# Output stages on VectorE alone, larger transfers and another spacing of attention bursts in a fused sparse-attention and max-feed-forward kernel

## The chip, the cores and the metric

One core of one Trainium2 chip. The metric is device time in microseconds for one execution; the kernel before was run three times, and one further execution was profiled. Besides PE (TensorE, with its weight loads PEld) the core has VectorE (DVE), ScalarE (ACT), GpSimd (POOL) and SyncE (SP), and 16 DMA engines.

## The reference

Attention with 8 batches, 8 heads, 576 positions and 64 channels, then a feed-forward layer with a maximum over three weights:

```python
mask_local = (rel >= 0) & (rel < stride)                      # heads 0..3, stride = 32
mask_strided = (rel >= 0) & (pos[None, :] % stride == pos[:, None] % stride)   # heads 4..7
attn = softmax(where(mask, scale * q @ k.T, -1e9))
x = (attn @ v).transpose(0, 2, 1, 3).reshape(4608, 512)
h = np.maximum(np.maximum(x @ w1, x @ w2), x @ w3)            # [4608, 768]
return h @ w_out                                              # [4608, 512]
```

All is float32.

## The kernel before

Float32 products are made of three products of parts: each operand is split into a high part (a cast, on ScalarE) and a low part (the operand less its high part, on VectorE or GpSimd), and PE adds high·high, high·low and low·high in a PSUM bank. There are two such banks, used in turn (`bank()`).

**Attention** goes by units: a unit is two heads of a batch, 32 units, in each batch two strided ones and then two local ones. A unit passes `scores` (PE), `less_maximum` (DVE), `exponentials` (ACT), `probabilities` and `transposed` (DVE), `values` (PE), and `leading` and `rest`, copies to the token blocks. `burst(n)` does the values of unit n, the scores of unit n+1, the v load of n+2, the copies of n, the q and k load of n+3, and the maximum of n+1. The rest of unit n+1 follows in the next steps. A strided unit's v comes in four transfers of 32 rows (L280).

**Tokens.** Chunk one (512 tokens) is in an opening whose order stands in a string of steps (`OPENING`). Chunk two (512 tokens; loop at L714) has 18 steps of a first product (`ff_in`, `ff_max`: j = i // 3, weight i % 3) and 4 of the output (`ff_out`, `ff_store`); `first_bursts` says which step begins with which burst. Beside it `build_sums`, `build_mix`, `build_high` and `build_low` make sums of weights, mostly on GpSimd, for nine quads in the DRAM tensor `scratch`; `sums_at` says when.

The other 3584 tokens go in four **supers**, each of two blocks of 448 tokens. A super has nine quads of seven products (a Strassen-like scheme; operands A11, S1, S2, S4, S3, A12, A22), so 63 products k = 0 to 62, each of six matmuls of 448 (`product`, L762). The weight operand of each product is a stream of 256 KB loads from `scratch`, issued by SP with nine buffers (`load_next`, L661). In supers 0 to 3, 6, 6, 4 and 0 bursts go between the products (`COUNTS`), at k = 0, 10, 20 and so on (`before`), and the rest of a unit's attention two to five products later (`after`). Between products ScalarE copies banks (`snap`, L800), GpSimd adds and VectorE takes the maxima into `h_all` (L814).

**The output stage** of a super has seven tiles of 128 tokens, 18 matmuls of 512 each (`out_part`, L847). For each, `split` makes the parts of h: the high one on ScalarE (L837), the low one mostly on GpSimd (L838); `store` copies the bank on ScalarE (L853) and sends it off on ScalarE's own DMA queue (L855). Between tiles stands a piece of `conversion(s + 1)`, which makes the seven operands of the next super's x: casts on ScalarE (L673), low parts on VectorE, two of them on GpSimd (L676), and four differences of blocks on VectorE (L679). Conversion 0 runs beside the output steps of chunk two, whose stores are at L557 and L558.

What sets the order: every engine works through its instructions in the order in which they are written (`pin`). SP issues all loads and the stores to `scratch`, in order; ScalarE issues the stores of the output. The compiled program has eight DMA semaphores, taken in turn over both queues: each transfer waits until the one eight before it has landed, and the engine that issues it waits with it.

Of the kernel before, what the change touches and what calls it, by code (L numbers as in the profile page):

```python
# [33 lines left out]
PAIRED = 1  # L34
# [37 lines left out]
def fused_kernel(ctx, tc, qT, kT, qk_loc, qk_str, v_loc, v_str, m_loc, m_str, w1, w2, w3, w_out, out):  # L72
# [183 lines left out]
    def load_v(n):  # L256
        if n >= len(units):
            return
        b, p = units[n]
        if n in (2, 3):  # L260
            vt = io_early.tile([P, 2 * (MB + 1) * D], F32, name="v_t", bufs=2)
        else:
            vt = io.tile([P, 2 * MS * D], F32, name="v_t", bufs=2)
        if p < 2:

            v_of[n] = v = vt[:, : 2 * (MB + 1) * D].rearrange("p (h m d) -> p h m d", h=2, m=MB + 1)
            last = 3 * MB
            for j in range(3):
                pin(nc.sync.dma_start(out=v[32 * j : 32 * (j + 1)], in_=v_loc[b, p, :32, :, j * MB : (j + 1) * MB + 1, :]))
                yield  # L270
            pin(nc.sync.dma_start(out=v[96:, :, : NT - last, :], in_=v_loc[b, p, :32, :, last:, :]))
            yield
            pin(nc.sync.dma_start(out=v[96:, :, NT - last, :], in_=v_loc[b, p, 32:, :, NT - 1, :]))
            yield
        else:
            v_of[n] = v = vt.rearrange("p (h m d) -> p h m d", h=2, m=MS)
            for j in range(4):

                rows = NI if b < PAIRED else 32
                pin(nc.sync.dma_start(  # L280
                    out=v[32 * j : 32 * j + rows], in_=v_str[b, p - 2, :rows, :, j * MS : (j + 1) * MS, :]
                ))
                yield
# [282 lines left out]
    def build_sums(q):  # L566

        _, j, i = builds[q]
        to = scratch[q].rearrange("p n (l f) -> p n l f", l=2)
        for n in range(2):  # L570
            pin(nc.sync.dma_start(out=to[:, A12 : A11 + 1, n], in_=halves(kept[i, j].bitcast(F32)[:, n])))
        pin(nc.sync.dma_start(out=to[:, A22], in_=kept[i, j + 1].bitcast(F32)[:, :, :256]))
        if q % 3 == 0:
            both = swp.tile([P, 2, 512], F32, name="sums_low")
            a = [both[:, n] for n in range(2)]
        else:
            a = [wk.tile([P, 512], F32, name="work") for _ in range(2)]
        a_of[q] = a
        for x, jj, engine in zip(a, (j, j + 1), (nc.gpsimd, nc.gpsimd)):
            parts = kept[i, jj].bitcast(F32)  # L580
            pin(engine.tensor_tensor(out=x, in0=parts[:, 0], in1=parts[:, 1], op=ALU.add))
# [31 lines left out]
    for step in LOADS.split():  # L613
        if step[0] == "w":
            load_weights(1)
        else:
            if step not in begun_loads:
                begun_loads[step] = {"q": load_qk, "v": load_v}[step[0]](int(step[1:]))
            next(begun_loads[step])
# [18 lines left out]

    def burst(n, exponents_later=True):
# [15 lines left out]
    def load_next():  # L657
        if to_load:
            _, q, m = to_load.pop(0)
            w = second["wst"].tile([P, 2, 256], F32R, name="w_stream")  # L660
            pin(nc.sync.dma_start(out=w.bitcast(F32), in_=scratch[q][:, m].rearrange("p (l f) -> p l f", l=2)))  # L661
            stream.append(w)

    half = lambda blk, k: blk[:, 2:4, :] if k == 1 else blk[:, 0:2, :]
# [1 line left out]
    def conversion(s):  # L666
# [5 lines left out]
        def high(m, src):  # L672
            pin(nc.scalar.copy(out=x[m][:, 0], in_=src))  # L673

        def low(m, src, engine=nc.vector):
            pin(engine.tensor_tensor(out=x[m][:, 1], in0=src, in1=x[m][:, 0].bitcast(F32), op=ALU.subtract))  # L676

        def less(to, a, b):
            pin(nc.vector.tensor_tensor(out=to, in0=a, in1=b, op=ALU.subtract))  # L679
# [26 lines left out]
    x1.close()  # L706
    late = ExitStack()
    shp.append(late.enter_context(tc.tile_pool(name="sums", bufs=2)))
    first_bursts = {1: 8, 4: 9, 6: 10, 9: 11, 12: 12, 14: 13, 17: 14, 19: 15}
    sums_at = {-2: 1, 0: 2, 3: 3, 5: 4, 7: 5, 9: 6, 11: 7, 14: 8}  # L710
    coming, since = None, 0
    convert = iter(())
    paired_queries(9)
    for i in range(3 * NJ + CH // P):  # L714
        if i in first_bursts:
            coming, since = burst(first_bursts[i]), i
        if i < 3 * NJ:
            ff_in(1, i // 3, i % 3)
        else:
# [2 lines left out]
            exponentials(coming)  # L722
        if coming and i == since + 1:
            probabilities(coming)
        if i < 3 * NJ:
            ff_max(1, i // 3, i % 3)
        else:
            ff_store(1, i - 3 * NJ)
        if coming and i == since + 1:
            transposed(coming)  # L730
            if (coming + 1) % 4 in (0, 1):
                paired_queries(coming + 1)
            coming = None
        if i >= 3 * NJ:
            next(convert, None)
            load_next()
            load_next()
        if i - 3 in sums_at:
# [17 lines left out]
    def supers():  # L756
# [9 lines left out]

        def before(s, k):

            if k % 10 == 0 and k // 10 < COUNTS[s]:
                running[:] = [burst(16 + sum(COUNTS[:s]) + k // 10), k]  # L770

        def after(s, k):

            if running and running[0]:
# [6 lines left out]
                if k == since + 5 and n + 1 < len(units) and (n + 1) % 4 in (0, 1):  # L781
                    paired_queries(n + 1)

        def quad(s, q):
# [45 lines left out]

        halves_of, outs = {}, {}

        def split(t, j0, j1, engine):
# [3 lines left out]
            pin(nc.scalar.copy(out=to[:, 0, j0:j1], in_=src))  # L837
            pin(engine.tensor_tensor(out=to[:, 1, j0:j1], in0=src, in1=to[:, 0, j0:j1].bitcast(F32), op=ALU.subtract))  # L838

        def out_part(t, j0, j1):  # L840
            if t not in outs:
# [16 lines left out]
        for s in range(NSUPER):  # L858
            for q in range(9):
                quad(s, q)  # L860
                if q == 7:
                    split(0, 0, 4, nc.gpsimd)
                    split(1, 0, 4, nc.gpsimd)
            split(2, 0, 4, nc.gpsimd)
            split(0, 4, 6, nc.vector)
            split(1, 4, 6, nc.vector)
            split(2, 4, 6, nc.gpsimd)
            convert = conversion(s + 1) if s + 1 < NSUPER else iter(())
            out_part(0, 0, 4)
            out_part(1, 0, 4)  # L870
            for t in range(7):
                out_part(t, 0 if t > 1 else 4, 6)
                store(s, t)
                if t < 4:
                    split(t + 3, 0, 6, nc.gpsimd)
                next(convert, None)
            list(convert)

# [67 lines left out]
```

## Time and profile before

| | |
|---|---|
| three runs | 712.08, 713.73, 712.32 us; median 712.32 us |
| profiled execution | 715.08 us, span of the core 713.3 us |
| PE busy | 657.0 us (92%) |
| VectorE busy | 374.7 us (53%) |
| ScalarE busy | 336.6 us (47%) |
| GpSimd busy | 379.2 us (53%) |
| mean granted clock of PE | 0.968 |
| DMA | 138.36 MB, 194 GB/s mean |

In the chain of the profile each row is a start, a length, and an engine with what it writes and the line; times are in us from the span's start. In the windows the columns are: the stretch and its length, then busy us of PE (and its instructions), PEld, DVE, ACT and POOL, the granted clock of PE, the busy share of the 16 DMA engines, and GB/s. In the table of waits: who waits on whom, the sum of the waits, how many, the longest. In the timeline the bracket holds the idle time ahead of a row and what released it.

### The profile page before, as it was taken

How to read it: one execution, taken by the hardware profiler on the slowest of the kernel's cores; microseconds unless marked ns; L12 is line 12 of the kernel's file. 1: busy time of each engine (PE TensorE's matmuls, PEld its weight loads, DVE VectorE, ACT ScalarE, POOL GpSimd, SP SyncE). 2: the span in 40 equal slices, each digit the busy share in tenths (PEclk: the TensorE clock that was granted, in tenths of full speed). 3: DMA queues.
4: the chain of work that ended last, by engine and by line, in shares of the span. 5: the costliest groups of instructions: out<-in, count | busy, mean ns of one | idle time of the engine just before them, and what ended most of it. 6: DMA issues, size and time to landing. Idle time of an engine off the chain costs nothing.

```text
span 713.3 us, 18073 instructions
## 1 busy us (share of the span) xinstructions
PE 657.0 (92%) x7408; PEld 563.7 (79%) x7408; DVE 374.7 (53%) x475; ACT 336.6 (47%) x702; POOL 379.2 (53%) x331
## 2 busy tenths in 40 slices
PE   4689999789886899999899999989999998999997
PEld 3467877668675788988689988868999986999986
DVE  5776955466655483845637474563733463124330
ACT  4766655334243445544445455443444543444541
POOL 8679997499850243356514335661434663444551
PEclk9689999999999899999999999999999998999999
DMA  9799136678896568783166788316667711777511
GB/s 292 187 293 355 41 95 213 204 243 258 278 310 205 182 227 268 247 263 97 54 229 225 236 260 282 111 46 208 208 187 218 217 57 60 213 217 218 150 45 60
DMA packets 89370, 138.36 MB, mean 194 GB/s; under 512 B 10152, under 2 KB 39592, under 8 KB 89288
## 3 DMA queue, kind: packets, MB, share of 16 engines
q1 hardware_dynamic: 84104, 127.76, 57.8%
q10 hardware_dynamic: 5184, 9.44, 3.5%
q8 instruction: 59, 0.97, 0.6%
q14 instruction: 23, 0.19, 0.1%
HBM read 111.21 MB, written 25.95 MB: 192 GB/s over the span
## 4 chain that ended last, share of the span: by engine, by line
PE 75%; DVE 8%; DMA 7%; issue 4%; ACT 3%; SPq 2%; POOL 1%; ACTq 0%; DVEq 0%
PE f_ps L762 44%; PE f_ps L847 11%; PE f_ps L522 11%; DMA w<-in_w 5%; DVE x_block L679 3%; DVE xc L676 3%; PE o_ps L470 2%; PE o_ps L441 2%; PE f_ps L552 2%; PE s_ps L318 2%; PE s_ps L340 2%; ACT xc L673 1%; DMA scratch<-work 1%; DMA qk_t<-in_qT 1%; DMA scratch<-w 1%
## 5 line engine op out<-in xcount | busy, mean ns | idle before, releaser
L762 PE MATMUL f_ps<-xc,w_stream 128*128 128x448 f32 x1512 | 315.7, 369 | 4.7 <-ACT snap L800 3.7
L762 PEld LDWEIGHTS f_ps<-xc,w_stream 128*128 128x128 f32 x1512 | 283.9, 189 | 31.4 <-ACT snap L800 6.0
L800 ACT COPY snap<-f_ps 128x448 f32<-128x448 f32 x240 | 128.0, 534 | 161.7 <-PE f_ps L762 161.1
L814 DVE TENSOR_TENSOR h_all<-h_all,snap 128x448 f32<-128x448 f32 x96 | 95.7, 1034 | 124.2 <-POOL snap L812 124.2
L812 POOL TENSOR_TENSOR snap<-snap 128x448 f32<-128x448 f32 x72 | 90.9, 1270 | 127.2 <-ACT snap L800 73.3
L847 PE MATMUL f_ps<-wNone,h_parts 128*128 128x512 f32 x504 | 122.1, 405 | 9.3 <-ACT work L853 9.3
L847 PEld LDWEIGHTS f_ps<-wNone,h_parts 128*128 128x128 f32 x504 | 98.5, 196 | 32.1 <-ACT work L853 11.2
L522 PE MATMUL f_ps<-xh,w 128*128 128x512 f32 x288 | 96.3, 407 | 2.2 <-ACT xh L495 2.2
L812 POOL TENSOR_TENSOR h_all<-snap 128x448 f32<-128x448 f32 x36 | 41.4, 1154 | 89.3 <-ACT snap L800 88.3
L838 POOL TENSOR_TENSOR h_parts<-h_all,h_parts 128x768 fp32r<-128x768 f32 (+2 forms) x32 | 56.0, 1755 | 45.9 <-ACT h_parts L837 45.4
L522 PEld LDWEIGHTS f_ps<-xh,w 128*128 128x128 f32 x288 | 55.9, 194 | 16.7 <-ACT xh L495 2.6
L522 PE MATMUL f_ps<-xl,w 128*128 128x512 f32 x144 | 57.9, 402 | 2.3 <-issue 2.1
L676 DVE TENSOR_TENSOR xc<-x_block,xc 128x896 fp32r<-128x896 f32 x20 | 32.9, 1646 | 38.9 <-ACT xc L673 34.0
L673 ACT CAST xc<-x_block 128x896 fp32r<-128x896 f32 x28 | 25.6, 940 | 30.0 <-DVE x_block L679 23.9
L361 DVE TENSOR_TENSOR s_ps<-s_ps,mloc 128x640 f32<-128x640 f32 x14 | 11.6, 829 | 47.3 <-PE s_ps L340 47.3
L853 ACT COPY work<-f_ps 128x512 f32<-128x512 f32 x28 | 16.3, 584 | 41.7 <-PE f_ps L847 41.7
L676 POOL TENSOR_TENSOR xc<-x_block,xc 128x896 fp32r<-128x896 f32 x8 | 22.2, 2774 | 23.5 <-ACT xc L673 23.5
L522 PEld LDWEIGHTS f_ps<-xl,w 128*128 128x128 f32 x144 | 28.1, 195 | 7.7 <-issue 1.5
L384 ACT ACTIVATE s_ps<-s_ps 128x640 f32<-128x640 f32 (+2 forms) x30 | 19.5, 649 | 30.7 <-DVE s_ps L368 30.7
L404 DVE STREAM_TRANSPOSE pt<-s_ps 128x640 f32<-128x640 f32 (+2 forms) x32 | 32.5, 1015 | 0.9
L361 DVE TENSOR_TENSOR s_ps<-s_ps,mpair 128x576 f32<-128x576 f32 x14 | 10.7, 763 | 42.0 <-PE s_ps L318 42.0
L837 ACT CAST h_parts<-h_all 128x768 fp32r<-128x768 f32 (+2 forms) x40 | 24.6, 644 | 17.2 <-DVE h_all L814 10.2
(89 smaller groups left out, 745.3 us busy)
## 6 DMA issues: line engine op xcount, KB each, us to landing
w_stream<-scratch SPq DMA_DIRECT2D x252, 256.0 KB
w<-in_w SPq DMA_DIRECT2D x18, 512.0 KB
out<-work ACTq DMA_DIRECT2D x36, 256.0 KB
qk_t<-in_qT SPq DMA_DIRECT2D x28, 288.0 KB
qk_t<-in_kT SPq DMA_DIRECT2D x28, 288.0 KB
v_t<-in_v_str SPq DMA_DIRECT2D x56, 128.0 KB
scratch<-w SPq DMA_DIRECT2D x27, 256.0 KB
v_t<-in_v_loc SPq DMA_DIRECT2D x48, 96.0 KB
```

The lines of the kernel that those rows point to most:

```text
L361: pin(nc.vector.tensor_tensor(out=flat, in0=flat, in1=mask.broadcast_to(list(flat.shape)), op=ALU.add))
L404: pin(nc.vector.transpose(pt[:, :, : nm * at], s_ps[:, :, : nm * at]))
L522: pin(nc.tensor.matmul(f_ps, w[:, kc, :], x[:, kc, :], start=(kc == 2 and n == 0), stop=(kc == 1 and n == 2)))
L673: pin(nc.scalar.copy(out=x[m][:, 0], in_=src))
L676: pin(engine.tensor_tensor(out=x[m][:, 1], in0=src, in1=x[m][:, 0].bitcast(F32), op=ALU.subtract))
L762: pin(nc.tensor.matmul(out_, w[:, wl, fs], x[:, xl, k, :], start=start and k == 0 and n == 0, stop=k == 1 and n == 2, skip_group_check=not ...
L800: pin(nc.scalar.copy(out=t, in_=src))
L812: pin(nc.gpsimd.tensor_tensor(out=h if i == 0 else u, in0=u, in1=t, op=ALU.add))
L814: pin(nc.vector.tensor_tensor(out=h, in0=h, in1=u, op=ALU.max))
L837: pin(nc.scalar.copy(out=to[:, 0, j0:j1], in_=src))
L838: pin(engine.tensor_tensor(out=to[:, 1, j0:j1], in0=src, in1=to[:, 0, j0:j1].bitcast(F32), op=ALU.subtract))
L847: pin(nc.tensor.matmul(outs[t], h, w, start=(j == 0 and n == 0), stop=(j == NJ - 1 and n == 2)))
```

## The change

1. `conversion` goes in six pieces and not four. All seven low parts are on VectorE (two were on GpSimd). ScalarE's casts of a piece read differences that VectorE took in the piece before.
2. `split` puts all low parts of h on VectorE.
3. The v of a strided unit from batch 1 on comes in one transfer of 512 KB; its source list begins with a dimension of four.
4. `build_sums` stores two operands with one contiguous 512 KB transfer in place of two strided ones of 256 KB; the loads of these two operands (A12 and A11, 72 of 252) then read two runs of 1 KB per partition, not one of 2 KB.
5. In chunk two, bursts 10 and 13 begin a step later; `transposed` stands ahead of `ff_max`; the last burst of the chunk (15) leaves out the scores and maximum of unit 16 and the q and k load of unit 18. These stand at product 1 of super 0. Conversion 0 is spread over the output steps as 2, 0, 1 and 1 pieces, the others after them.
6. In the supers, bursts stand at k = 8, 18, and so on to 58. The queries of a strided unit are prepared four products after its burst, not five. (`ahead` is called by nothing.)

```diff
+            if b >= PAIRED:
+                src = v_str[b, p - 2, :32].rearrange("r h (j m) d -> j r h (m d)", j=4)
+                pin(nc.sync.dma_start(out=vt.rearrange("p (h x) -> p h x", h=2), in_=src))
+                yield
+                return
...
-        for n in range(2):
-            pin(nc.sync.dma_start(out=to[:, A12 : A11 + 1, n], in_=halves(kept[i, j].bitcast(F32)[:, n])))
+        pin(nc.sync.dma_start(out=scratch[q][:, A12 : A11 + 1].rearrange("p n x -> p (n x)"), in_=kept[i, j].bitcast(F32).rearrange("p l x -> p (l x)")))
...
+            if m in (A12, A11):
+                src = scratch[q][:, A12 : A11 + 1].rearrange("p l (n f) -> p n l f", n=2)[:, m]
...
-        coming = n + 1 if n + 1 < len(units) else None
+        coming = n + 1 if n + 1 < len(units) and not alone else None
...
         high(A11, b11)
+        high(A12, b21)
         low(A11, b11)
-        high(A12, b21)
-        low(A12, b21, nc.gpsimd)
+        low(A12, b21)
         yield
         less(b11, b12, b11)
-        high(S1, b11)
-        low(S1, b11)
         yield
         high(S4, b22)
+        high(S1, b11)
+        low(S4, b22)
         less(b12, b22, b12)
-        low(S4, b22)
+        yield
         less(b22, b22, b11)
+        low(S1, b11)
+        high(S3, b12)
+        yield
         high(S2, b22)
+        low(S3, b12)
+        less(b21, b21, b22)
+        yield
+        high(A22, b21)
         low(S2, b22)
-        yield
-        high(S3, b12)
-        less(b21, b21, b22)
-        high(A22, b21)
-        low(S3, b12, nc.gpsimd)
         low(A22, b21)
...
-    first_bursts = {1: 8, 4: 9, 6: 10, 9: 11, 12: 12, 14: 13, 17: 14, 19: 15}
+    first_bursts = {1: 8, 4: 9, 7: 10, 9: 11, 12: 12, 15: 13, 17: 14, 19: 15}
...
-            if k % 10 == 0 and k // 10 < COUNTS[s]:
+            if s == 0 and k == 1:
+                scores(16)
+                list(load_qk(18))
+                less_maximum(16)
+                running[:] = [16, k]
+            elif k % 10 == 8 and k // 10 < COUNTS[s]:
...
-            pin(engine.tensor_tensor(out=to[:, 1, j0:j1], in0=src, in1=to[:, 0, j0:j1].bitcast(F32), op=ALU.subtract))
+            pin(nc.vector.tensor_tensor(out=to[:, 1, j0:j1], in0=src, in1=to[:, 0, j0:j1].bitcast(F32), op=ALU.subtract))
```

How this moves instructions, first on VectorE in the output stage between supers 2 and 3. In these rows `h_all` are maxima of h, `h_parts` low parts of h, `xc_…` low parts of x and `x_block_…<-` differences. Before:

```order
L814 TENSOR_TENSOR h_all<-h_all,snap 128x448 x16
L838 TENSOR_TENSOR h_parts<-h_all,h_parts 128x256 x2
L676 TENSOR_TENSOR xc_7156<-x_block_5090,xc_7156 128x896
L679 TENSOR_TENSOR x_block_5090<-x_block_6143,x_block_5090 128x896
L676 TENSOR_TENSOR xc_7157<-x_block_5090,xc_7157 128x896
L679 TENSOR_TENSOR x_block_6143<-x_block_6143 128x896
L676 TENSOR_TENSOR xc_7159<-x_block_6143,xc_7159 128x896
L679 TENSOR_TENSOR x_block_6143<-x_block_6143,x_block_5090 128x896
L676 TENSOR_TENSOR xc_7158<-x_block_6143,xc_7158 128x896
L679 TENSOR_TENSOR x_block_5090<-x_block_5090,x_block_6143 128x896
L676 TENSOR_TENSOR xc_7162<-x_block_5090,xc_7162 128x896
```

And after, at the same place (the last row is not the end of the stage):

```order
L835 TENSOR_TENSOR h_all<-h_all,snap 128x448 x4
L859 TENSOR_TENSOR h_parts<-h_all,h_parts 128x512
L859 TENSOR_TENSOR h_parts<-h_all,h_parts 128x256 x3
L859 TENSOR_TENSOR h_parts<-h_all,h_parts 128x768
L689 TENSOR_TENSOR xc_7105<-x_block_5128,xc_7105 128x896
L689 TENSOR_TENSOR xc_7110<-x_block_5128,xc_7110 128x896
L859 TENSOR_TENSOR h_parts<-h_all,h_parts 128x768
L692 TENSOR_TENSOR x_block_5128<-x_block_6174,x_block_5128 128x896
L859 TENSOR_TENSOR h_parts<-h_all,h_parts 128x768
L689 TENSOR_TENSOR xc_7108<-x_block_6174,xc_7108 128x896
L692 TENSOR_TENSOR x_block_6174<-x_block_6174 128x896
L859 TENSOR_TENSOR h_parts<-h_all,h_parts 128x768
```

The low parts of h, 128x768 each, now stand on VectorE between the pieces of the conversion, and no piece there alternates any more between a difference and the low part of that same difference.

Second, ScalarE from the second output tile of chunk two into super 0. `work` and the DMA of `out` are a tile's copy and store, `xc_…` a cast of the conversion. Before:

```order
L557 COPY work<-f_ps_790 128x512
L558 DMA out<-work 128x512
L673 CAST xc_2967<-x_block_1139 128x896
L557 COPY work<-f_ps_791 128x512
L558 DMA out<-work 128x512
L295 COPY pt<-qk_t 128x2x8x18 x2
L295 COPY pt<-qk_t 128x2x8x14 x2
L673 CAST xc_2969<-x_block_1909 128x896
L673 CAST xc_2968<-x_block_1909 128x896
L557 COPY work<-f_ps_790 128x512
L558 DMA out<-work 128x512
```

And after:

```order
L562 COPY work<-f_ps_784 128x512
L563 DMA out<-work 128x512
L562 COPY work<-f_ps_785 128x512
L563 DMA out<-work 128x512
L686 CAST xc_2939<-x_block_1894 128x896
L686 CAST xc_2937<-x_block_1133 128x896
L562 COPY work<-f_ps_784 128x512
L563 DMA out<-work 128x512
L686 CAST xc_2940<-x_block_1894 128x896
L686 CAST xc_2938<-x_block_1894 128x896
L686 CAST xc_2942<-x_block_1133 128x896
```

The copies of queries (`pt<-qk_t`) have left this place, the second and third store follow each other directly, and three of the casts stand behind the last store.

Third, PE from the last output tile of chunk two into super 0 (`f_ps<-xc` is a product, `o_ps` the values of a unit, `s_ps` scores). Before:

```order
L552 MATMUL f_ps_790<-wNone_1526,hl 128x512
L470 MATMUL o_ps<-pt,v_t 64x2x18 x32
L318 MATMUL s_ps<-qk_t,pt 64x2x18 x32
L762 MATMUL f_ps_791<-xc_2966,w_stream 128x448 x6
L762 MATMUL f_ps_790<-xc_2967,w_stream 128x448 x6
L762 MATMUL f_ps_791<-xc_2968,w_stream 128x448 x6
```

And after:

```order
L557 MATMUL f_ps_784<-wNone_1520,hl 128x512
L778 MATMUL f_ps_785<-xc_2936,w_stream 128x448 x6
L323 MATMUL s_ps<-qk_t,pt 64x2x18 x32
L778 MATMUL f_ps_784<-xc_2937,w_stream 128x448 x6
L778 MATMUL f_ps_785<-xc_2938,w_stream 128x448 x6
```

Values of unit 16 and scores of unit 17 have left the place between the last output tile and the first product; the scores of unit 16, which stood an output tile or more earlier, now stand behind the first product.

More of the change, by code (lines that the diff above doesn't have):

```diff
@@ L637, in fused_kernel, with ahead, burst @@
             list(load_v(n + 2))
-    def burst(n, exponents_later=True):
+    def ahead(n):
+        if n < len(units):
+            scores(n)
+            list(load_qk(n + 2))
+    def burst(n, alone=False):
         values(n)
-        coming = n + 1 if n + 1 < len(units) else None
+        coming = n + 1 if n + 1 < len(units) and not alone else None
         if coming:
@@ L673, in high, with low @@
             pin(nc.scalar.copy(out=x[m][:, 0], in_=src))
[L675 to L676 removed]
+        def low(m, src):
+            pin(nc.vector.tensor_tensor(out=x[m][:, 1], in0=src, in1=x[m][:, 0].bitcast(F32), op=ALU.subtract))
         def less(to, a, b):
@@ L715, in fused_kernel @@
         if i in first_bursts:
-            coming, since = burst(first_bursts[i]), i
+            coming, since = burst(first_bursts[i], first_bursts[i] == 15), i
         if i < 3 * NJ:
@@ L734, in fused_kernel @@
         if i >= 3 * NJ:
-            next(convert, None)
+            for _ in range((2, 0, 1, 1)[i - 3 * NJ]):
+                next(convert, None)
             load_next()
```

28 lines of the change are left out of this document (15 added, 13 removed).

## The prediction

> **What bounds the kernel now.** I read the page first, then the chain that ended last, then the windows and the timeline of the places where the chain leaves PE. The page's first line gives the span; the profiled execution took 715.08 us and the median of the runs shown is 712.32, so every sum below is made against 715.08 and multiplied by 712.32/715.08 = 0.9961 at the end.
>
> ```profile
> span 713.3 us, 18073 instructions
> ...
> 325.15 6.84 PE f_ps L847 x30
> ...
> 358.83 1.07 PE o_ps L441 x66
> ...
> 451.16 6.84 PE f_ps L847 x30
> ...
> 484.83 1.07 PE o_ps L470 x64
> ...
> 569.24 6.84 PE f_ps L847 x30
> 576.11 0.60 ACT work L853
> 577.90 0.95 ACT xc L673
> 578.87 2.04 DVE xc L676
> 580.93 2.91 DVE x_block L679
> 592.21 0.59 ACT work L853
> 592.84 11.23 PE f_ps L847 x36
> 604.08 76.61 PE f_ps L762 x378
> 680.69 28.59 PE f_ps L847 x126
> ```
>
> These are pieces of the chain (start, length, what). In the product stages (L762) it is PE alone. In the first three output stages (L847) it leaves PE for ScalarE and VectorE, and in the last one, which has no conversion beside it, it stays on PE: 126 matmuls in 28.59 us. The others last, from start to the first work of the next stage, 358.83 − 325.15 = 33.68, 484.83 − 451.16 = 33.67 and 604.08 − 569.24 = 34.84 us. Against 28.59 they lose 5.09 + 5.08 + 6.25 = 16.42 us. The timeline (start, length, engine; in brackets the idle time ahead and its releaser) and a window tell how:
>
> ```profile
> 578.87 2.03 DVE L676 TENSOR_TENSOR xc<-x_block,xc 128x896 fp32r<-128x896 f32 x1 [4.86 <-ACT xc L673]
> ...
> 592.33 1.09 DVE L676 TENSOR_TENSOR xc<-x_block,xc 128x896 fp32r<-128x896 f32 x1 [1.00 <-ACT xc L673]
> ```
> ```profile
> 572.81 1.02 ACT L837 CAST h_parts<-h_all 128x256 fp32r<-128x256 f32 x3 [2.48 <-DVE h_all L814]
> ...
> 591.36 0.94 ACT L673 CAST xc<-x_block 128x896 fp32r<-128x896 f32 x1 [3.98 <-DVE x_block L679]
> ```
> ```profile
> 593.00:597.00 4.00, 4.00 (x10) 3.17 (x11) 2.68 (x3) 3.00 (x4) 2.89 (x2) 0.50 0.21 70
> ```
>
> ScalarE stands 3.98 us before a cast because VectorE has not finished the difference that it reads; the bank's copy (592.21) is queued behind that cast, and PE waits for the copy. Right after it, PE's granted clock is 0.50. VectorE's same operation takes 2.03 us while GpSimd works and 1.09 when it doesn't.
>
> **The output stages.** GpSimd leaves them, ScalarE's casts read differences of the piece before, and VectorE takes all low parts. What VectorE then has is 11 operations of the conversion at 1.09 = 12.0 us, and 4 full low parts of h:
>
> ```profile
> L838 DVE TENSOR_TENSOR h_parts<-h_all,h_parts 128x256 fp32r<-128x256 f32 x8 | 3.0, 422 | 1.9 <-ACT h_parts L837 1.9
> ...
> L838 POOL TENSOR_TENSOR h_parts<-h_all,h_parts 128x768 fp32r<-128x768 f32 x16 | 35.3, 2207 | 35.0 <-ACT h_parts L837 35.0
> ```
>
> The trace has no 768-element low part on VectorE. Between 0.422 (256 elements) and 1.09 (896) I take, in a straight line, 0.96; 2.2 is the upper end, GpSimd's. 4 × 0.96 = 3.8, together 15.8 of 28.6 us of PE work: covered. The cover ends when the 15 operations take over 28.6/15 = 1.91 us each. Next in line is ScalarE: seven copies at 0.59, four casts of 768 and seven of 896 at under 0.95, about 14.6 us, also covered. So the 16.42 go. Given back: the bursts now stand at product 58 in the first two supers, so VectorE comes to the last maxima of h later, and the casts already wait 2.48 us for these (row 572.81). I put 0.5 us to each of the two, at most 2.48. Term: −16.4 + 1.0 = **−15.4** (−16.4 to −11.4).
>
> **Chunk two and the join into the first super.** In chunk two the chain shows these losses:
>
> ```profile
> 180.71 2.12 issue
> ...
> 194.60 2.48 POOL work L581 x2
> ...
> 205.18 7.87 DMA scratch<-work
> 213.74 5.11 DMA qk_t<-in_qT
> ```
> ```profile
> PE o_ps L441 <- ACT hh L542: 1.6, 1, 1.6
> ```
>
> The other spacing, and the transposition ahead of the maximum, can take away those two (3.7 us) and puts bursts two steps apart at two other places, where I price about 0.85 each from them; −2. But from 194 on the chain is GpSimd's sums and their stores, which the change does not shorten: a PE that is early then waits. At the join:
>
> ```profile
> 224.69 1.18 PE L470 MATMUL o_ps<-pt,v_t 64*64 64x36 f32 x62 [3.29 <-DVE pt L404]
> ...
> 225.71 1.15 PE L318 MATMUL s_ps<-qk_t,pt 64*64 64x36 f32 x62
> ...
> 234.44 12.67 PE L762 MATMUL f_ps<-xc,w_stream 128*128 128x448 f32 x48 [3.72 <-ACT snap L800]
> ```
> ```profile
> 218.93 0.34 ACTq L558 DMA_DIRECT2D out<-work  x1
> 219.31 0.95 ACT L673 CAST xc<-x_block 128x896 fp32r<-128x896 f32 x1 [5.69 <-DMA qk_t<-in_qT]
> ```
>
> A store on ScalarE's queue waits until the transfer eight places before it in the program has landed; here that is unit 18's q, and casts, copies and then PE stand behind it. After, that load is at product one and does not gate it: 2 × 288 KB at the 384 GB/s of the row below is −1.5 us. The third store now waits for unit 17's v in its place. How long that takes depends on one thing, the number of DMA engines that carry it:
>
> ```profile
> 208.00:212.00 4.00, 4.00 (x55) 3.32 (x48) 3.64 (x5) 2.13 (x8) 2.19 (x1) 1.00 1.06 384
> 360.00:451.00 91.00, 90.50 (x1166) 81.01 (x1154) 49.89 (x69) 46.86 (x108) 35.13 (x28) 1.00 0.78 253
> 600.00:681.00 81.00, 81.00 (x399) 74.51 (x398) 22.43 (x22) 35.48 (x67) 35.54 (x29) 1.00 0.62 182
> ```
> ```profile
> v_t<-in_v_str SPq DMA_DIRECT2D x56, 128.0 KB
> ```
>
> The last two columns are the busy share of 16 engines and GB/s. A busy engine moves 384/16 = 24 GB/s where none idles, 253/(16 × 0.78) = 20.3, and 182/(16 × 0.62) = 18.3. The four transfers of 128 KB, whose lists begin with 32 rows, become one of 512 KB whose list begins with four groups. If the work is dealt out by that first dimension, four engines carry it, 131 KB each: 5.5 us at 24 GB/s, where 16 take 1.4. No view of before shows how many engines a transfer used; I take four, the dearer end. The Trainium skill, "DMA: Bandwidth & Descriptors", section "Why a DMA increments its semaphore by 16 and not by 1", says that the number of engines is the largest one up to 16 that divides the slowest dimension of both access patterns. By that rule it would be four here, so it speaks against this part of the change; with 16 the sum would be that of the first rival.
>
> With four, v16 and v17 add 4.1 us each: the third store goes at 218.9 − 1.5 + 8.2 = 225.6. Behind it come two casts and the fourth copy, and VectorE's four operations to S1's low part: S1 at about 231 and S2 at 234.5, as before (234.44), while the 2.3 us of burst 16 (rows 224.69 and 225.71) are still to be done at product 8. Join +2.3, of which I keep +2. If v16's surplus has drained by then it is −2; with 16 engines, S2 at 226.4, −8 + 2.3 and some 3 us of low clock less, −9. Both parts together: **0** (−11 to +6).
>
> **The opening.**
>
> ```profile
> 35.39 2.49 SPq L280 DMA_DIRECT2D v_t<-in_v_str  x4
> ```
> ```profile
> 45.59 0.65 PE L522 MATMUL f_ps<-xh,w 128*128 128x512 f32 x1 [2.17 <-ACT xh L495]
> ```
>
> SP spends 2.49 us on the four issues of v4, ahead of weight loads that ScalarE is waiting for; one issue saves 1.9. Over four engines the transfer then holds up the weights' share there by 4.1. The ends are −1.9 and +2.2; I take **+1**, nearer to the second since I took four engines.
>
> **The product stages.** The weight stream (256 KB each) now reads 72 of 252 blocks in two pieces of 1 KB. Its row 600 to 681 has the DMA at 0.62 with PE never idle, so it hides until such a block costs over twice as much. Six strided v loads fall here. From one burst to the next are
>
> ```profile
> 249.08 12.35 PE f_ps L762 x60
> 263.81 12.60 PE f_ps L762 x60
> ```
>
> 263.81 − 249.08 = 14.7 us. In that time each of the four engines has ten weight blocks (10 × 16.4 KB), q and k (36.9 KB) and v (131 KB), 332 KB: 13.8 us at 24 GB/s, 16.3 at 20.3, 18.1 at 18.3. So the lateness of each is 0, 1.6 or 3.4 us, 0 to 20 over six. I take the first, as the engine in question has no gaps then, and **+1.5** for uneven arrival. One transfer for two in the sums' stores, the unused helper and the earlier queries: nothing, since SP and the stores keep the same bytes and the queries still precede their scores.
>
> Sum: −15.4 + 0 + 1 + 1.5 = −12.9; 715.08 − 12.9 = 702.2, × 0.9961 = **699.4**.
>
> **Rivals.** *All sixteen engines carry the merged load.* For it: the other side of the copy has 128 partitions, enough for all. Against: the first list has only four entries. Then −15.4 − 10 − 1.9 + 0 = −27.3: 687.8, × 0.9961 = 685.1. Chance 0.14.
>
> *Four engines at the lower rate starve PE* (the slower side). For it: 20.3 and 18.3 in the very stages concerned. Against: these stretches have gaps, and nine weight buffers stand ahead. At 18.3 the products lose 20, the join 3.4 more (two loads at 7.2 for 5.5), the opening 1.7 more: −15.4 + 3.4 + 2.7 + 20 = +10.7: 725.8, 723.0 scaled. It decides against the change from about 2.1 us late per load, so 332 KB in 16.8 us, under 20 GB/s. Chance 0.17.
>
> *VectorE becomes the bound of the output stages.* For it: it gets all of GpSimd's work there and its own rows reach 2.03 and 2.91. Against: these rows stand beside GpSimd, which is now gone. At their mean, 2.47, 15 operations take 37.0 us against 34.1 now (the mean of the three stages): +9 instead of −15.4, with +2.5 from the rest 726.6, 723.8 scaled. The gain is gone at 34.1/15 = 2.27 us each. Chance 0.05.
>
> *It does not do what it says*, because a piece still waits on its neighbour: 715 or so. Chance 0.02.
>
> **The numbers.** The forecast has 0.62. A measurement of this kernel tells 0.3%, 2.1 us, from no change: faster is under 710.2, slower above 714.5. Faster: the forecast 0.60, sixteen engines 0.14, a mild starving 0.05, VectorE short of its bound 0.01, together 0.80. Slower: starving 0.08 and VectorE 0.03, together 0.11. Within: 0.09. The range takes in the join's and the products' bounds, half of the sixteen-engine case, and the mild part of the starving: 686 to 712.
>
> **What would show it.** Right: three output stages of 28.6 to 29.5 us, no wait of L853's kind on PE, VectorE's 896-element operations near 1.09 and the 768-element ones near 0.96, a clock of 1.00 at the start of the next products; S2 near 234 and the third store of chunk two waiting for v. Wrong: output stages of over 33 us with a busy VectorE; PE waiting for the weight stream one or two products after a strided burst (starving); S2 of the first super before 228 (sixteen engines).

## The result and the profile after

The changed kernel takes 734.67 us, the median of four runs (730.95 to 740.55), against 713.03 us (712.08 to 714.82) for the kernel before in the same comparison: 1.0308 times as long, with a 95% interval of 1.0236 to 1.0380. The forecast was 699.4 us and its range ended at 712: the change is slower, by about 21.6 us. The profiled execution took 740.55 us, the longest of the four, with a span of 738.8 us. Times of single places below come from one profiled execution of each kernel. Ratios here and below are of fast runs alone; one run of x8_before_spacing and one of x10_out_rows, its profiled one, were in a slower state.

First the output stages. These are pieces of the chain after (start, length, what), and then two rows of its groups (the last numbers ahead of the idle time are busy us and mean ns of one):

```profile
379.91 9.73 PE f_ps L778 x48
...
516.26 9.72 PE f_ps L778 x48
...
601.27 28.59 PE f_ps L868 x126
```
```profile
L689 DVE TENSOR_TENSOR xc<-x_block,xc 128x896 fp32r<-128x896 f32 x28 | 29.8, 1087 | 25.8 <-ACT xc L686 25.8
...
L859 DVE TENSOR_TENSOR h_parts<-h_all,h_parts 128x768 fp32r<-128x768 f32 x16 | 15.3, 959 | 26.0 <-ACT h_parts L858 25.7
```

The third output stage is one unbroken piece on PE, 28.59 us where it was 34.84. VectorE's operations take 1.09 and 0.96 us without GpSimd beside them. This part of the change did what it should.

The loss is elsewhere. The next rows are from PE's timeline after: the first matmul behind the wait of the opening, the first and the third product of super 0, and the starts of its first three output stages.

```profile
52.41 0.79 PE L527 MATMUL f_ps<-xh,w 128*128 128x512 f32 x1 [7.51 <-ACT xh L500]
...
232.35 1.49 PE L778 MATMUL f_ps<-xc,w_stream 128*128 128x448 f32 x6
...
247.72 10.05 PE L778 MATMUL f_ps<-xc,w_stream 128*128 128x448 f32 x36 [1.18 <-ACT snap L821]
...
350.39 5.65 PE L868 MATMUL f_ps<-wNone,h_parts 128*128 128x512 f32 x24
...
486.49 5.62 PE L868 MATMUL f_ps<-wNone,h_parts 128*128 128x512 f32 x24
...
601.11 28.75 PE L868 MATMUL f_ps<-wNone,h_parts 128*128 128x512 f32 x126
```

At 45.59 before, PE had waited 2.17 us; now it waits 7.51 and goes on at 52.41. S2 starts at 247.72 in place of 234.44. What PE and ScalarE wait for stands in the tables of waits (sum, times, longest) and in ScalarE's timeline at the join, and the chain names the transfers themselves:

```profile
PE f_ps L778 <- DMA w_stream<-scratch: 14.1, 4, 4.6
...
PE f_ps L527 <- ACT xh L500: 7.5, 1, 7.5
```
```profile
219.25 0.34 ACTq L563 DMA_DIRECT2D out<-work  x1
...
231.71 0.59 ACT L562 COPY work<-f_ps 128x512 f32<-128x512 f32 x1 [7.02 <-DMA w_stream<-scratch]
238.69 0.34 ACTq L563 DMA_DIRECT2D out<-work  x1
239.07 1.78 ACT L686 CAST xc<-x_block 128x896 fp32r<-128x896 f32 x2 [6.77 <-DMA v_t<-in_v_str]
```
```profile
128.62 9.41 DMA v_t<-in_v_str
...
225.98 12.63 DMA v_t<-in_v_str
...
290.39 13.24 DMA w_stream<-scratch
303.76 4.24 PE f_ps L778 x12
...
323.65 4.04 PE f_ps L778 x12
...
405.31 3.86 PE f_ps L778 x12
...
426.25 4.21 PE f_ps L778 x12
```

Behind the first store of chunk two, at 219.25, ScalarE waits twice. The first wait, 7.02 us by the profile for a weight block, holds the second store. The third store does wait for unit 17's v, as foretold, but that load takes 12.63 us, and the store goes at 238.69 and not at 225.6. In super 0 a weight block that is issued behind a v load lands 13.24 us after its issue. PE has run out of its nine buffers by then; before, PE never waited for the stream. And the 12 matmuls after the wait take 4.24 us, where 60 of them took 12.35 before, so that 12 took 2.5. The four waits for the stream stand behind the two strided v loads of super 0 and the first two of super 1, and the 12 matmuls after each take 3.86 to 4.24 us, together 6.5 more than at 2.5. The last two of the six v loads, in super 1 at 460.79 and 479.33, are followed by no such wait. The window after the first wait has the clock, third from the end, at 0.79:

```profile
303.00:311.00 8.00, 7.24 (x165) 6.44 (x166) 0.77 (x1) 1.96 (x7) 0.00 (x0) 0.79 0.60 197
```

### The profile page after: what moved, and what is told of

Its sections match the earlier page's. It is cut to its first block, busy times and chain, and to the rows that moved or that the text cites. A ratio compares the mean times of both kernels' runs of the same rounds, so it can differ in the third digit from the quotient of the medians.

```text
span 738.8 us, 17982 instructions
## 1 busy us (share of the span) xinstructions
PE 667.8 (90%) x7408; PEld 571.8 (77%) x7408; DVE 375.7 (51%) x515; ACT 336.4 (46%) x702; POOL 300.7 (41%) x291
## 4 chain that ended last, share of the span: by engine, by line
PE 68%; DMA 18%; issue 4%; DVE 3%; SPq 3%; ACT 2%; POOL 1%; ACTq 1%; DVEq 0%; POOLq 0%
PE f_ps L778 35%; PE f_ps L868 14%; PE f_ps L527 12%; DMA w_stream<-scratch 7%; DMA w<-in_w 4%; DMA v_t<-in_v_str 4%; PE o_ps L475 2%; PE s_ps L345 2%; PE s_ps L323 2%; DMA qk_t<-in_qT 1%; PE o_ps L446 1%; SPq L246 1%; DVE h_all L835 1%; ACTq L563 1%; POOL snap L833 1%
## 5 line engine op out<-in xcount | busy, mean ns | idle before, releaser
L778 PE MATMUL f_ps<-xc,w_stream 128*128 128x448 f32 x1512 | 326.0, 376 | 25.3 <-DMA w_stream<-scratch 14.1
L778 PEld LDWEIGHTS f_ps<-xc,w_stream 128*128 128x128 f32 x1512 | 289.9, 193 | 55.0 <-issue 17.4
L835 DVE TENSOR_TENSOR h_all<-h_all,snap 128x448 f32<-128x448 f32 x96 | 82.9, 906 | 119.1 <-POOL snap L833 118.9
L868 PE MATMUL f_ps<-wNone,h_parts 128*128 128x512 f32 x504 | 115.7, 390 | 1.1 <-ACT h_parts L858 1.1
L868 PEld LDWEIGHTS f_ps<-wNone,h_parts 128*128 128x128 f32 x504 | 94.3, 188 | 21.7 <-ACT h_parts L858 1.9
L527 PE MATMUL f_ps<-xh,w 128*128 128x512 f32 x288 | 100.3, 422 | 7.5 <-ACT xh L500 7.5
L527 PEld LDWEIGHTS f_ps<-xh,w 128*128 128x128 f32 x288 | 58.6, 204 | 21.6 <-ACT xh L500 7.9
L689 DVE TENSOR_TENSOR xc<-x_block,xc 128x896 fp32r<-128x896 f32 x28 | 29.8, 1087 | 25.8 <-ACT xc L686 25.8
L859 DVE TENSOR_TENSOR h_parts<-h_all,h_parts 128x768 fp32r<-128x768 f32 (+2 forms) x40 | 27.2, 712 | 26.0 <-ACT h_parts L858 25.7
L366 DVE TENSOR_TENSOR s_ps<-s_ps,mloc 128x640 f32<-128x640 f32 x14 | 11.6, 831 | 48.0 <-PE s_ps L345 46.2
L874 ACT COPY work<-f_ps 128x512 f32<-128x512 f32 x28 | 16.4, 587 | 41.8 <-PE f_ps L868 41.8
L527 PEld LDWEIGHTS f_ps<-xl,w 128*128 128x128 f32 x144 | 29.5, 205 | 6.6 <-DVE xl L505 0.6
L345 PE MATMUL s_ps<-qk_t 64*32 64x64 f32 (+1 forms) x1408 | 20.2, 232 | 14.5 <-DMA qk_t<-in_kT 7.6
L557 PE MATMUL f_ps<-wNone,hh 128*128 128x512 f32 x96 | 31.6, 411 | 0.0
```

What stands on the lines that cost most here:

```text
L345: pin(nc.tensor.matmul(s_ps[32 * j : 32 * (j + 1), h, k1 : k1 + w], t[hs, q0 : q0 + 32], t[hs, k0 : k0 + w], start=not first, stop=not fir ...
L527: pin(nc.tensor.matmul(f_ps, w[:, kc, :], x[:, kc, :], start=(kc == 2 and n == 0), stop=(kc == 1 and n == 2)))
L557: pin(nc.tensor.matmul(f_ps, h[:, ts], w, start=(j == 0 and n == 0), stop=(j == NJ - 1 and n == 2)))
L689: pin(nc.vector.tensor_tensor(out=x[m][:, 1], in0=src, in1=x[m][:, 0].bitcast(F32), op=ALU.subtract))
L778: pin(nc.tensor.matmul(out_, w[:, wl, fs], x[:, xl, k, :], start=start and k == 0 and n == 0, stop=k == 1 and n == 2, skip_group_check=not ...
L835: pin(nc.vector.tensor_tensor(out=h, in0=h, in1=u, op=ALU.max))
```

## The experiments

Theory: the merged load is carried by four engines, since its list begins with four groups; each is slower than I took it to be, and what SP issues behind it waits for it. Rivals: a transfer of 512 KB is slow by its size, however it is dealt out; or the loss comes from the other parts (spacing, 1 KB reads, stores).

**Four transfers again (x1_four), two transfers (x2_two), one of 128 rows (x3_rows), the merged load alone (x4_before_merged).** The first three are the changed kernel with one edit, the fourth is the kernel before with the merged load only.

```diff
 x1_four:
-            if b >= PAIRED:  (the merged load)
-                rows = NI
+                rows = NI if b < PAIRED else 32
 x2_two:
-                pin(nc.sync.dma_start(out=vt.rearrange("p (h x) -> p h x", h=2), in_=src))
+                for half in range(2):
+                    to = vt[64 * half : 64 * half + 64].rearrange("p (h x) -> p h x", h=2)
+                    pin(nc.sync.dma_start(out=to, in_=src[2 * half : 2 * half + 2]))
 x3_rows:
-                src = v_str[b, p - 2, :32].rearrange("r h (j m) d -> j r h (m d)", j=4)
-                pin(nc.sync.dma_start(out=vt.rearrange("p (h x) -> p h x", h=2), in_=src))
+                pin(nc.sync.dma_start(out=vt, in_=v_rows[b, p - 2]))
```

In x3_rows `v_rows` is a copy of the same v with the 128 partitions as its first dimension, laid out with the other inputs before the launch.

> The changed kernel with the strided v in four transfers of 128 KB again, all else as changed. Four engines (the merged load is slow because its list of four groups puts it on few DMA engines): that cost is gone and the output stages' gain stays, 695 to 703 us. Size (a transfer of 512 KB holds up the queue as a whole, however it is dealt out): the same, 695 to 703. Elsewhere (the loss comes from the burst spacing, the 1 KB reads or the stores of the sums): 725 us or more.

> The changed kernel with the strided v in two transfers of 256 KB, each of whose lists begins with two groups. Four engines: it is now two engines per transfer, 262 KB for each of them and load where it was 131, so slower than the changed kernel's 735 us, 755 us or more. Size: each transfer is half as large, so between four transfers and one, 710 to 725. Elsewhere: 735, unchanged.

> The changed kernel with the strided v in one transfer of 512 KB, from a copy of v laid out by partition beforehand, so that its list begins with 128 rows; same bytes, same runs or longer. Four engines: 16 engines carry it, 690 to 700 us. Size: 735, unchanged. Elsewhere: 725 or more.

> The kernel before with nothing but the strided v merged into one transfer of 512 KB with a list of four groups. Four engines and size: the whole loss without the gain of the output stages, 730 to 752 us. Elsewhere: 711 to 716, no change.

Measured, all against 713.23 us for the kernel before: x1_four 698.45 us, ratio 0.9783 (0.9738 to 0.9827); x2_two 800.21 us, 1.1207 (1.1132 to 1.1281); x3_rows 693.55 us, 0.9717 (0.9681 to 0.9752); x4_before_merged 761.28 us, 1.0629 (1.0557 to 1.0700). x1_four came out as both theories had it: without the merged load the rest of the change is faster than the kernel before, and the merged load costs 36 us on top of it. Halving the transfers made them worse by 65 us, and 512 KB in one transfer of 128 rows is the fastest of the four, so size falls; the merged load alone is slower than the whole change, so "elsewhere" falls. PE's timeline of x3_rows at the places shown above:

```profile
44.59 0.50 PE L526 MATMUL f_ps<-xh,w 128*128 128x512 f32 x1 [1.00 <-ACT xh L499]
...
217.05 1.39 PE L777 MATMUL f_ps<-xc,w_stream 128*128 128x448 f32 x6
...
222.77 9.26 PE L777 MATMUL f_ps<-xc,w_stream 128*128 128x448 f32 x36 [1.84 <-ACT snap L820]
...
313.88 5.63 PE L867 MATMUL f_ps<-wNone,h_parts 128*128 128x512 f32 x24
...
439.98 5.62 PE L867 MATMUL f_ps<-wNone,h_parts 128*128 128x512 f32 x24
...
554.48 28.75 PE L867 MATMUL f_ps<-wNone,h_parts 128*128 128x512 f32 x126
```

The two kernels differ in nothing but this load (in x3_rows it also reads runs of 4 KB and not 2 KB; x5_eight and x6_alone below speak to that), so the differences are its price, place by place:

| up to | after | 128 rows | behind by | added here |
|---|---|---|---|---|
| the opening's wait | 52.41 | 44.59 | 7.8 | 7.8 |
| first product | 232.35 | 217.05 | 15.3 | 7.5 |
| third product | 247.72 | 222.77 | 24.9 | 9.6 |
| output stage of super 0 | 350.39 | 313.88 | 36.5 | 11.6 |
| of super 1 | 486.49 | 439.98 | 46.5 | 10.0 |
| of super 2 | 601.11 | 554.48 | 46.6 | 0.1 |

The last strided v loads are issued in super 1 (unit 29 with burst 27), and behind them nothing is added. The profiled execution of the changed kernel was its longest, so the 46.6 us are more than the 41.1 between the medians.

x4_before_merged lost 48 us, more than the change gives back in the output stages, and lies above the 752 us expected at most. Two rows of its waits on PE:

```profile
PE f_ps L767 <- DMA w_stream<-scratch: 21.5, 6, 4.8
PE o_ps L475 <- DVE pt L409: 14.2, 3, 11.8
```

The second is 0.2 us in the changed kernel. The values of a strided unit stand in the join there and wait, 11.8 us ahead of the first product; that the change's other spacing is what spares it this wait is argued from the order, no run shows it.

**Eight groups (x5_eight).** The changed kernel, with v from a copy laid out in eight groups of 16 rows with a gap between groups, so that the groups don't merge into one dimension.

```diff
-                src = v_str[b, p - 2, :32].rearrange("r h (j m) d -> j r h (m d)", j=4)
-                pin(nc.sync.dma_start(out=vt.rearrange("p (h x) -> p h x", h=2), in_=src))
+                pin(nc.sync.dma_start(out=vt, in_=v_rows[b, p - 2, :, :16]))   # v_rows: [B, 2, 8, 17, 1024]
```

> The changed kernel with the strided v in one transfer of 512 KB whose list begins with eight groups (from a copy laid out beforehand with a gap between groups). Number of engines decides, and they are eight: each carries 66 KB of a load, with the stream 266 KB in 14.7 us, 18 GB/s; if an engine reaches that, as good as 128 rows, 692 to 700 us; if one engine stays near the 13 GB/s of the changed kernel's first v load in a super, 705 to 725. Size decides: 735.

It took 706.26 us, ratio 0.9865 (0.9815 to 0.9915). With lists that begin with 2, 4, 8 and 128 the same bytes give ratios of 1.1207, 1.0308, 0.9865 and 0.9717, in the order of the number of groups. Eight is not yet as good as 128, though both read runs of 4 KB: the second case of the expectation.

**The loads alone (x6_alone)**, one after the other, with nothing beside them:

```diff
+    for n in range(N):
+        src = v_str[n, 0].rearrange("r h (j m) d -> j r h (m d)", j=4)
+        pin(nc.sync.dma_start(out=t.rearrange("p (h x) -> p h x", h=2), in_=src))
+        use(t)        # VectorE reads a column, so that the next load waits
```

> Only loads, one after the other with nothing beside them; it leaves out the whole computation and stores zeros. Six each of: 512 KB with a list of four groups, of 128 rows and of eight groups, 256 KB of two groups, four of 128 KB together, a block of 256 KB, and a 512 KB load of four groups with four blocks right behind it. An engine moves 24 GB/s whatever the list: four groups land 4 us after the same bytes by 128 rows, about 7 against 3 us, two groups as four. An engine alone is slower: four groups take 10 us or more, eight about half, and the blocks behind a load of four groups land after it and not before. Size: all 512 KB loads alike.

The chain of this kernel has each load from its issue to its landing; one of each form, then windows in the middle of one load of four groups, of 128 rows, of eight and of two groups (here the columns are the stretch, its length, DVE, POOL, PEclk, DMA share, GB/s):

```profile
27.52 8.36 DMA v_four<-in_v_str
...
58.85 3.24 DMA v_rows<-in_v_rows
...
83.89 6.11 DMA v_eight<-in_v_eight
...
123.17 7.80 DMA v_two<-in_v_str
...
166.86 3.13 DMA v_parts<-in_v_str
...
187.09 2.80 DMA block<-in_v_rows
...
228.59 10.90 DMA behindd<-in_v_rows
```
```profile
30.00:34.00 4.00, 0.00 (x0) 0.00 (x0) 1.00 0.26 88
60.40:61.20 0.80, 0.00 (x0) 0.00 (x0) 1.00 1.00 394
86.00:89.00 3.00, 0.00 (x0) 0.00 (x0) 1.00 0.44 152
125.00:130.00 5.00, 0.00 (x0) 0.00 (x0) 1.00 0.13 47
```

512 KB land after 8.36 us by four groups, 6.11 by eight and 3.24 by 128 rows; four groups lie between the two cases of the expectation. 256 KB by two groups take 7.80, about as long as twice the bytes by four: it is the bytes per group that count. It isn't the pattern in memory either, since `v_parts`, four transfers that read the same 2 KB runs, has landed 3.13 us after its last issue and 5.0 after its first. In the middle of a load the busy share of 16 engines is 0.26 for four groups, 4.2 engines; 1.00 for 128 rows, 16; 0.44 for eight, 7.0; and 0.13 for two, 2.1. The Trainium skill, "DMA: Bandwidth & Descriptors", section "Why a DMA increments its semaphore by 16 and not by 1", has the rule by which these are 4, 16, 8 and 2 engines; the trace agrees to within one engine.

A block of 256 KB lands after 2.80 us alone and, as the last of four behind a load of four groups, 10.90 us after its own issue. From the first and second row, (131 − 33 KB)/(8.36 − 3.24 us) is 19 GB/s for the further bytes of one engine's share, over a whole load with its start and end. In the middle the windows have more: 88 GB/s by four engines is 22 each, 394 by 16 is 25. So the 24 that I had taken is near the pace of an engine with nothing beside it. Eight groups don't lie on this line (33 KB more than 128 rows cost 2.9 us), and I have no reason for it.

**The output stages alone (x7_before_out) and the spacing alone (x8_before_spacing)**, each put into the kernel before. x7 has the new `conversion` and `split`; x8 has

```diff
-    first_bursts = {1: 8, 4: 9, 6: 10, 9: 11, 12: 12, 14: 13, 17: 14, 19: 15}
+    first_bursts = {1: 8, 4: 9, 7: 10, 9: 11, 12: 12, 15: 13, 17: 14, 19: 15}
...
-            if k % 10 == 0 and k // 10 < COUNTS[s]:
+            if s == 0 and k == 1:
+                scores(16)
...
+            elif k % 10 == 8 and k // 10 < COUNTS[s]:
```

with `transposed` ahead of `ff_max` and the queries one product earlier.

> The kernel before with the new conversion and split alone (parts 1 and 2). The term of the output stages as forecast: 713 - 15.4 = 697.6, so 696 to 702 us. If part of that gain came from the other spacing instead: 703 to 710.

> The kernel before with the new burst spacing, the earlier transposition and the scores of unit 16 in the first super (parts 5 and 6, without the six pieces of the conversion). Forecast with v on 16 engines: 10 us less at the join, 703. If the join is held by the stores of the sums anyway: 710 to 714. If bursts at product 58 hold up the output stages that still use GpSimd: 714 to 720.

x7 took 695.35 us against 715.38, ratio 0.9713 (0.9667 to 0.9759). Its chain has every output stage whole:

```profile
325.56 28.61 PE f_ps L849 x126
...
446.56 28.58 PE f_ps L849 x126
...
559.67 28.61 PE f_ps L849 x126
```

Its span is 697.1 us, 16.2 below the one of before, where the forecast's term without the give-back was 16.4; by the medians it is 20.0, just below the range expected. x8 took 714.53 us against 715.38, ratio 0.9981 (0.9954 to 1.0009): no change that can be told, the middle case, and not the 10 us less of the forecast with v on 16 engines. Its profiled execution, the fastest of ten, has S2 at 228.68, 5.8 us earlier than before, so the join was shorter in that one; where the others lose this, no trace shows.

**The old sums (x9_rows_old_sums), the best of the parts (x10_out_rows), 128 rows alone (x11_rows_alone).** x9 is x3_rows with part 4 undone; x10 is x7 with v by 128 rows; x11 is the kernel before with v by 128 rows. The edits are those shown.

> The changed kernel with v by 128 rows (as in the run of that name) and with the stores of the sums as before, so the weight blocks are read in runs of 2 KB again (part 4 undone). If part 4 costs nothing, as forecast: 691 to 696 us, as with part 4 (693.6). If reads of 1 KB cost something beside the stream: 685 to 690.

> The kernel before with the output stages of the change and v by 128 rows, without parts 4 to 6. Output stages alone gave 695; one issue in place of four gives the opening's 1.9 back and the join up to 5: 688 to 693 us. If the larger gain at the join needs the new spacing: 693 to 696, above the changed kernel with 128 rows.

> The kernel before with nothing but v by 128 rows. Opening 1.9 us and up to 5 at the join: 706 to 711 us. If the transfers' number didn't matter: 712 to 715.

Against 712.03 us: x9 690.57 us, ratio 0.9711 (0.9646 to 0.9776), the same as x3_rows with 0.9717, so part 4 costs nothing that can be told; the time itself lies between the two ranges expected. The windows 600 to 650 of the two show PE without a gap in both:

```profile
600.00:650.00 50.00, 50.00 (x248) 46.33 (x248) 14.88 (x16) 21.86 (x41) 22.02 (x18) 1.00 0.75 217
```
```profile
600.00:650.00 50.00, 50.00 (x249) 46.33 (x248) 14.69 (x16) 21.88 (x41) 20.95 (x19) 1.00 0.75 216
```

x11 took 703.49 us, 0.9882 (0.9836 to 0.9928): one wide transfer for four narrow issues is worth 8.5 us by itself, more than I had expected. x10 took 687.06 us, ratio 0.9629 (0.9567 to 0.9692), just below the range expected and better than both kernels. Whether parts 4 to 6 cost something beside it isn't settled, as its interval overlaps that of x3_rows. The traces show one place for it. From the first output stage to the second x3_rows has 126.1 us (313.88 to 439.98) and x7, with the old spacing, 121.0 (325.56 to 446.56). In x3_rows PE stands 1.93 us inside the scores of one burst there, and the products behind it are slow:

```profile
417.51 14.21 PE L777 MATMUL f_ps<-xc,w_stream 128*128 128x448 f32 x60
```

The other 60 matmuls between two bursts of this super take 12.4 to 12.7 us. The changed kernel and x9 have the same wait and the same slow products; x8, with the old output stages, waits 0.45 us there and takes 12.60. So by these runs it comes with the new spacing and the new output stages together; why the scores wait is not shown.

**Two queues (x12_queues).** The load of four groups and four blocks behind it again, on SP's queue, and then with the large load on ScalarE's queue:

```diff
+    for name, queue in (("v_same", nc.sync), ("v_other", nc.scalar)):
...
+            pin(queue.dma_start(out=v.rearrange("p (h x) -> p h x", h=2), in_=src))
```

> Only loads again; it leaves out the whole computation and stores zeros. Six times a 512 KB load of four groups with four blocks of 256 KB right behind it, all on SP's queue, then six times the same with the large load on ScalarE's queue. If the blocks wait because they are behind it in one queue: 11 us to the first block in the first form, 3 to 5 in the second, and the large load lands after the blocks. If the four engines' total is what counts: 10 us or more in both.

VectorE reads the four blocks, and then v. Its timeline in the first form and in the second:

```profile
29.83 0.15 DVE L20 COPY seen<-blocka 128x1 f32<-128x1 f32 x1 [10.96 <-DMA blocka<-in_v_rows]
...
31.96 0.15 DVE L20 COPY seen<-v_same 128x1 f32<-128x1 f32 x1
```
```profile
113.88 0.15 DVE L20 COPY seen<-v_other 128x1 f32<-128x1 f32 x1 [11.25 <-DMA v_other<-in_v_str]
114.07 0.15 DVE L20 COPY seen<-blocka 128x1 f32<-128x1 f32 x1
```

In one queue VectorE waits 10.96 us for the first block, and v is there when it comes to read it. In the second form the two rows belong to one load and the next: VectorE waits 11.25 us for v, and the next four blocks, which SP issued at 102.09 to 103.46, just behind that v on the other queue (101.91), are there already. The window in the second half of this stretch (columns as in the windows of x6_alone) tells more:

```profile
108.00:112.00 4.00, 0.00 (x0) 0.00 (x0) 1.00 0.26 100
```

A share of 0.26 is that of one load of four groups by itself, so the blocks have moved by 108, at most 6 us after their issue. So in one queue the blocks come after the load, in two before it, and it is the place in the queue that makes them wait for all of it. Whether they land within the 3 to 5 us expected stays open, since VectorE's order of reads hides it; the load itself takes longer there, 11.9 us from issue to landing where four groups alone took 8.36. Whether the kernel would gain from a second queue wasn't tried.

## Why the prediction was wrong

**Output stages, −15.4: right.** The durations were right to 0.01 us (1.09, and 0.959 for the estimate of 0.96). The third stage lasts 28.59. The first two last 379.91 − 350.39 = 29.5 and 516.26 − 486.49 = 29.8, so 0.9 and 1.2 were given back, not 0.5 each: 14.3 in all.

**Chunk two and the join, 0: the join came out about so, chunk two did not.** These are the first stores of chunk two, before and in x3_rows; after, it is at 219.25.

```profile
205.70 0.34 ACTq L558 DMA_DIRECT2D out<-work  x1
```
```profile
203.99 0.34 ACTq L562 DMA_DIRECT2D out<-work  x1
```

From there to S2 it is 28.7 us before (to 234.44), 18.8 in x3_rows (to 222.77) and 28.5 after (to 247.72). So in these single traces the new spacing took 10 us from the join and the load by four groups gave them back, near the −8 (S2 at 226.4) and +8.2 of the forecast. The mechanism was in part the one named: the third store waits for unit 17's v and S2 waits behind it. The 7.02 us that the second store waits for a weight block were not in it. But S2 was to start at 234.5 and started at 247.72, since the first store was already 13.6 us late; that is the opening and what follows it, below. And in whole times the spacing alone gave nothing that can be told (x8).

**The opening, +1: too small.** PE's wait grew from 2.17 to 7.51 us, and PE goes on 6.8 us later than before (52.41 against 45.59). My upper end was +2.2.

**The product stages, +1.5: this is the step that failed most.** It said that "each of the four engines has" 332 KB between two bursts, "13.8 us at 24 GB/s", and took that rate "as the engine in question has no gaps then". Against 128 rows the load cost 11.6 and 10.0 us in supers 0 and 1, 21.6 together. Four of the six loads were late, by 5.8 us each in super 0 and 5.0 in super 1. Of the 21.6, 14.1 are PE's waits for the stream and 6.5 the slow matmuls behind them, which the term did not have at all. With 5.8 us more, the 332 KB took 14.7 + 5.8 = 20.5 us, an estimate of 16 GB/s for an engine. Alone, one engine does reach 22 to 25 GB/s in the middle of such a load (88 GB/s by four in x6_alone, 100 in x12_queues). It is beside the stream that it doesn't: the last section has a stretch of super 0 without gaps in which the 16 engines moved 12 GB/s each. So "no gaps" did not mean 24. The second rival had 20 for this, from the 18.3 GB/s row, at 3.4 us for each of six loads; that four loads at more came to about the same is luck. I had the number and gave it 0.17, because I held the 24 of a stretch with all 16 engines at work to be the pace of an engine whatever stands beside it.

Super 1 lost 4.3 us more than this load explains: its products last 106.6 us (379.91 to 486.49) and 92.3 before (358.83 to 451.16). The forecast had nothing there; the slow products shown with x10 stand in the same place.

**Between the opening and the first product** I had priced nothing of this load, and it cost 7.5 us more; the chain shows one such load, 9.41 us at 128.62. With the second rival's own price, 723.0, this and the opening were still missing.

**The sixteen-engine rival** named the right remedy, and 685.1 was its price. The changed kernel with 128 rows took 693.55 and x10 687.06, so its time was nearly reached only without the other spacing; the stretch of super 1 shown with x10 is some 5 us of it.

**The 1 KB reads, the stores: nothing, right** as far as x9 can tell, whose interval is about 5 us to either side.

The chances were wrong in the same place. That four engines carry the load was taken as given in 0.79 of the cases, and then it was only a matter of one rate whether the change is a gain or a loss. The two rates, 24 and 18.3, lay on both sides of the 20 at which it turns, and nothing in the trace of before showed one narrow load beside the stream, so there was no reason strong enough for 0.62 against 0.17.

## What to carry to other kernels

Merging transfers saves issues, but look at the first dimension of the merged list: with four groups, 512 KB took 8.4 us, with 128 rows 3.2, and the stream queued behind it starved PE. Where a price hangs on the pace of one engine, neither a total rate divided by the busy engines nor such a load timed by itself gives it: here an engine moved 22 GB/s alone and about 16 beside the stream. Try that one load in the kernel. And measure the parts of a change apart: here one part gained 16 to 20 us, one 8.5 if laid out by 128 rows, and the same part laid out by four groups lost 48.

## What was not expected of the hardware

The busy share of the DMA engines is not a measure of what they move. These windows are of super 0, after (beside a v load of four groups) and in x3_rows:

```profile
292.00:301.00 9.00, 8.61 (x42) 7.43 (x40) 5.34 (x8) 5.77 (x13) 3.49 (x3) 1.00 1.06 189
```
```profile
257.00:261.00 4.00, 4.00 (x22) 3.68 (x20) 0.89 (x2) 1.64 (x4) 2.48 (x3) 1.00 1.06 388
```

At the same share of 1.06, all 16 engines busy, one stretch moves 189 GB/s, 12 for each engine, and the other 388, 24 for each. The four-group load alone moved 88 GB/s at a share of 0.26. So beside the stream the narrow load does not leave the other twelve engines looking idle: all of them count as busy, at half the pace. Why they are slower is not shown.
